# A delta rule, then Fourier mixing and an MLP, on one core: MLP pieces recorded inside the first mixing, and fewer beside the last batch's chain

## The chip, the cores and the metric

The kernel runs on one core of a Trainium2 chip. The metric is the device time of one execution in microseconds (us). Six runs are given, and their median is the number that a change is held against. One further execution was profiled; its trace is what is read below.

The core's engines run side by side, each through its own instruction list in order, and wait for one another by semaphores. In the profile PE is TensorE (matmuls, with PEld its weight loads), DVE is VectorE, ACT is ScalarE, POOL is GpSimd, and SP is the engine that issues most DMA transfers.

## The reference

Two blocks follow each other, on 4 batches, 8 heads, 768 rows and a head dimension of 48 (so 384 columns):

```python
k_n = k / (np.linalg.norm(k, axis=-1, keepdims=True) + 1e-06)
for t in range(S):
    y[:, :, t] = np.einsum('bhd,bhde->bhe', q[:, :, t], state)
    v_old = np.einsum('bhde,bhd->bhe', state, kt)
    state = state + bt[:, :, :, None] * np.einsum('bhd,bhe->bhde', kt, vt - v_old)
...
X = np.fft.fft(x, axis=1)
X = np.fft.fft(X, axis=2)
mixed = np.real(X).astype(np.float32)
u = x + mixed
un = (u - mu) / np.sqrt(var + 1e-06)
ch = np.maximum(un @ w_ch1, 0.0) @ w_ch2
return (u + ch).astype(np.float32)
```

The second block takes `y` with the heads side by side as `x`. The two weights (384 x 1536 and 1536 x 384) come as 64-bit floats, and the kernel turns them into 32-bit ones itself. All arithmetic is in 32-bit floats; a matmul of this kind is two records in the trace.

## The kernel before

**The recurrence as a chain.** Rows are taken in chunks of 64: 12 chunks to a batch, 48 chain steps in all (`chain`, L657). A step is three rounds that each need the one before: products of the state with the keys (`pc<-st`) and a subtraction on DVE (`U<-V,pc`); products with a small triangular inverse (`pc<-U,wt`) and a copy on ACT (`U<-pc`); products with the keys (`pc<-U,kp`) and an addition on DVE (`st<-st,pc`). After every second step `outputs` (L715) forms 128 rows of the first block's result in `x` (`py` products, an ACT copy, a DVE addition).

**Ahead of the chain.** Four steps are a quad, eight a group. For each group `prepare` (L413) transposes keys and queries (`pt`) and forms their products (`pg`), `invert` (L500) inverts 32 x 32 triangles for 128 partitions at once on DVE (a transpose into `X`, some 60 small operations named `A<-X` and `X<-X,A`, then `Y`, `Z` and a transpose back into `A`), and `merge` (L626) joins them into the `wt` tiles by `pj` products and ACT copies. A step can't use its `wt` before its group is merged.

**Behind the chain.** `fourier` (L777) mixes a finished batch: folds on DVE and POOL (into `hT` or `scr`, and `F`), products with the Fourier tables (`pf`), an ACT copy into `F`, then for each of three tiles the products `pb`, six DVE additions into `x`, the statistics (`bst`, `mv`) and the reciprocal deviation `rstd` on POOL; the third tile has one more product, `pd`. Each `yield` in it ends one recorded step. The first mixing has 15 such steps, a later one 13. When a tile's `rstd` is recorded, its key stands in `norms`. `mlps` (L900) is the MLP, over twelve pairs (batch, tile) in a row: normalise into `un` (DVE), transpose (`ptr`, ACT copy into `unT`), 12 pieces of three `ph` matmuls with an ACT copy into `hT`, 12 pieces of two `po` matmuls in two rows, each row closed by a DVE addition into `x` and a store. Each yield is a recorded step. A step comes back empty when the next pair isn't in `norms`, or when the second weight isn't yet converted for the next `po` (`converted`). The second weight's conversion (`second_weight`, L358) uses ACT (`digits`, L300), two DVE operations and one on POOL per piece of 128 rows, with three stage buffers that DMAs on SP refill.

**What sets the order.** Up to chain step 11 the order is written out by hand (`strict[0] = True`). From L1096 on, a scheduler at build time orders each engine's list, by the order of recording as priority and by which inputs and buffers it holds ready; at run time each list is followed as built. So what the main loop (L1131 to L1172) records earlier tends to stand earlier. Beside each chain step it adds to two counters. Each of the three rounds adds `PRE` (or 4.6 for the first group) to the one for the preparation of the next group, and `SIDE[b]` to the one for the MLP; when that one reaches 1, `beside` (L1123) records one step of the current mixing, if one is under way, and one MLP step. While a step waits to be merged, `beside` is called as well. After the last step the last mixing is begun and `beside` is called until all is recorded. The first mixing's two first steps are recorded beside chain steps 10 and 11, its other 13 in one go at chain step 12, by `run(first_mixing)` (L1154).

The PSUM buffers named "one" (two of them) serve `pt`, `ptr`, `pf`, `pb`, `pd`, `ph` and `po` in turn.

Of the kernel before, what the change touches and what calls it, by code (L numbers as in the profile page):

```python
# [82 lines left out]
def kernel(  # L83
# [542 lines left out]
    def merge(g):  # L626

        for lh in range(2):
            M = Merge(g, lh)
            for step in range(2):  # L630
                for half in range(2):
                    M.products(step, half)
                yield "ACT"
                M.taken(step, vs=(0,))
                yield "ACT"
                M.taken(step, vs=(1,))
                for hh in range(2):
                    yield ("ACT", "DVE")[step]
                    M.diagonal(step, hh, *((), (dve.tensor_copy,))[step])
                if step == 0:  # L640
                    yield
            merged.add(2 * g + lh)
            yield
# [110 lines left out]
    def advancing(gens):  # L754

        if gens and next(gens[0], "end") == "end":
            gens.pop(0)
# [17 lines left out]
    norms = {}  # L775
# [192 lines left out]
    def advance(gen, n=1):  # L968
        for _ in range(n):
            if next(gen, "end") == "end":  # L970
                return False
        return True

    def run(*gens):
        for gen in gens:
            for _ in gen:
                pass
# [5 lines left out]
    def queries(*Qs):  # L983
        for Q in Qs:
            while Q >= NB and Q - NB in held:
                yield
            yield from prepare(Q, (1,))
# [69 lines left out]
    first_mixing = fourier(0)  # L1057
# [40 lines left out]
    def kept(gen):  # L1098

        while True:  # L1100
            strict[0] = True
            more = advance(gen)
            strict[0] = False
            if not more:
                return
            yield

    def ahead(g):
        if g == 2:
            yield from kept(queries(4, 5))  # L1110
        for Q in (2 * g, 2 * g + 1):
            while Q >= NB and Q - NB in held and g > 2:
                yield
            if g > 2:
                yield from prepare(Q)
        yield from invert(g)
        for _ in merge(g):
            yield

    mixing = [None]  # L1120
    channels = mlps()

    def beside():  # L1123

        if mixing[0] is not None:
            if not advance(mixing[0]):
                mixing[0] = None
        return advance(channels)


    PRE, SIDE = 2.4, (0.0, 1.5, 2.2, 2.2)  # L1131
    pre, due = ahead(2), [0.0, 0.0]
    for m in range(NCH, STEPS):
        b, n = divmod(m, NCH)
        g, Q = m // (2 * QT), m // QT

        count = 0
        while Q not in merged:
            advance(pre)
            count += 1  # L1140
            if count % 3 == 0 and b > 1 or count % 4 == 0 and len(converted) == KF:
                beside()
        if m % (2 * QT) == 1:
            run(pre)
            pre = ahead(g + 1) if g + 1 < NG else iter(())
            due = [0.0, 0.0]
        for i, _ in enumerate(chain(m)):
            if i < 2:
                advancing(later)
            if n == 0 and i == 1:  # L1150
                run(*later)
                later.clear()
                if b == 1:
                    run(first_mixing)  # L1154
                else:
                    mixing[0] = fourier(b - 1)
            if b == 1 and (n > 0 or i > 1):
                advance(second, 3)
            if m > NCH or i > 0:
                due[0] += 4.6 if g == 1 else PRE  # L1160
                due[1] += SIDE[b]
            while max(due) >= 1.0:
                if due[1] >= 1.0:
                    due[1] -= 1.0
                    beside()
                if due[0] >= 1.0:
                    due[0] -= 1.0
                    advance(pre)
# [34 lines left out]
```

## Time and profile before

| what | value |
|---|---|
| median of six runs | 777.41 us (773.63 to 780.0) |
| profiled execution | 773.58 us, span 771.9 us |
| mean granted PE clock | 0.982 of full speed |
| `ph` matmuls | 864 records, 209.9 us busy |
| `po` matmuls | 576 records, 209.3 us busy |
| chain step 12 / 16 / 36 / 40 / 47, first product | 153.3 / 215.6 / 489.2 / 554.2 / 629.1 us |

The span runs from the first to the last instruction; the execution's own time has a little around it. The page gives busy time by engine, the chain of waits that ended last, and groups of instructions; windows give the same busy times for a stretch, and a timeline lists instructions in order with, in brackets, the idle time before one and what ended it. The granted clock is the share of full speed that PE's clock was given: matmuls take longer where it is below 1. A busy PE is not the same as a PE at full speed, and idle time on an engine that nothing waits for costs nothing.

### The profile page before, as it was taken

The numbers are of one execution on the slowest core, as the hardware profiler recorded it, in microseconds if no ns is written. First come the engines' busy times: TensorE is split into PE (matmuls) and PEld (weight loads), VectorE is DVE, ScalarE is ACT, GpSimd is POOL, SyncE is SP. The second block draws the span as 40 slices with busy tenths as digits, with TensorE's granted clock in tenths as the row PEclk, the third lists the DMA queues.
The fourth block names the chain that finished last, engine by engine and source line by source line (L and its number), as shares of the span: only waits on it lengthen the run. The fifth ranks groups of instructions, "written<-read, shape, count | busy, mean of one in ns | idle before, by whom it ended". The sixth has DMA issues, their size and how long they took to land.

```text
span 771.9 us, 18290 instructions
## 1 busy us (share of the span) xinstructions
PE 678.7 (88%) x7768; PEld 486.1 (63%) x7768; DVE 395.6 (51%) x980; ACT 258.1 (33%) x700; POOL 80.5 (10%) x116
## 2 busy tenths in 40 slices
PE   5934598887979898899999999899999999799996
PEld 4622477665746665766766667567667676577683
DVE  2599776889972597344894123889211114600000
ACT  3742355543336414523313544113522122121120
POOL 8010023323000000000100000101000001100000
PEclk9999999998999999999999999899999999899999
DMA  8642032343112201002202010000100000000000
GB/s 182 166 108 50 6 85 65 87 141 74 31 27 49 45 14 44 11 12 42 48 11 48 7 33 17 16 11 11 23 23 2 21 2 21 0 1 21 10 11 20
DMA packets 81041, 30.78 MB, mean 40 GB/s; under 512 B 75856, under 2 KB 77392, under 8 KB 80960
## 3 DMA queue, kind: packets, MB, share of 16 engines
q1 hardware_dynamic: 76560, 21.92, 13.3%
q0 software_dynamic: 2224, 7.31, 2.9%
q8 instruction: 61, 1.00, 0.5%
q10 hardware_dynamic: 2176, 0.39, 0.3%
q14 instruction: 20, 0.16, 0.1%
HBM read 24.87 MB, written 4.72 MB: 38 GB/s over the span
## 4 chain that ended last, share of the span: by engine, by line
PE 54%; DVE 26%; ACT 6%; DMA 5%; SPq 4%; issue 3%; POOL 1%; POOLq 0%; DVEq 0%; ACTq 0%
PE ph L131 18%; PE po L131 17%; DVE A L131 6%; DVE X L131 5%; PE pc L131 5%; DVE x L131 3%; DVE w L131 3%; PE pf L131 3%; ACT A L131 2%; PE pj L131 2%; PE pg L131 2%; PE pt L131 2%; SPq L219 2%; DMA qp<-in_q_dram 2%; PE pb L131 2%
## 5 line engine op out<-in xcount | busy, mean ns | idle before, releaser
L131 PE MATMUL ph<-unT,w 128*128 128x256 f32 x864 | 209.9, 392 | 2.8 <-DVE x L131 1.4
L131 PE MATMUL po<-w,hT 128*128 128x384 f32 x576 | 209.3, 504 | 0.0
L131 PEld LDWEIGHTS ph<-unT,w 128*128 128x128 f32 x864 | 160.4, 192 | 30.7 <-ACT unT L131 2.2
L131 PEld LDWEIGHTS po<-w,hT 128*128 128x128 f32 x576 | 103.9, 192 | 61.1 <-issue 4.1
L131 ACT ACTIVATE hT<-ph 128x256 f32<-128x256 f32 x144 | 55.0, 382 | 189.3 <-PE ph L131 189.1
L131 DVE TENSOR_TENSOR x<-x,po 128x384 f32<-128x384 f32 x24 | 13.2, 552 | 95.4 <-PE po L131 95.3
L131 PE MATMUL pg<-KQT 48*64 48x64 f32 (+1 forms) x1152 | 45.1, 299 | 6.4 <-ACT KQT L131 4.6
L770 POOL DMA_INDIRECT out_dram<-x,rows_hi x12 | 12.3, 1026 | 353.8 <-DVE x L131 223.0
L131 DVE TENSOR_TENSOR U<-V,pc 128x192 f32<-128x192 f32 x48 | 16.7, 348 | 63.4 <-PE pc L131 63.4
L131 PEld LDWEIGHTS pg<-KQT 48*64 48x64 f32 x1152 | 34.6, 180 | 22.9 <-ACT KQT L131 12.3
L131 ACT ACTIVATE KQT<-pt 128x256 f32<-128x256 f32 (+1 forms) x84 | 33.0, 413 | 45.7 <-PE pt L131 44.8
L131 DVE TENSOR_TENSOR X<-X,A 128x30 f32<-128x30 f32 (+14 forms) x120 | 40.7, 339 | 3.2
L131 DVE TENSOR_TENSOR A<-X 128x30 f32<-128x30 f32 (+14 forms) x120 | 39.6, 330 | 3.1
L131 DVE TENSOR_TENSOR st<-st,pc 128x192 f32<-128x192 f32 x44 | 15.4, 350 | 49.5 <-PE pc L131 31.5
L131 ACT ACTIVATE U<-pc 128x192 f32<-128x192 f32 x48 | 15.8, 329 | 65.5 <-PE pc L131 62.1
L131 PE MATMUL pt<-pack,qp 128*128 128x128 f32 x96 | 23.7, 344 | 15.5 <-DMA qp<-in_q_dram 12.1
L131 PEld LDWEIGHTS pc<-U,wt 64*64 64x64 f32 x768 | 20.9, 154 | 22.9 <-DVE U L131 9.2
L131 PE MATMUL pc<-U,wt 64*64 64x48 f32 x768 | 28.0, 250 | 7.5 <-DVE U L131 5.5
L131 PEld LDWEIGHTS pc<-st,KQT 48*64 48x64 f32 x768 | 18.9, 157 | 24.8 <-DVE st L131 11.8
L131 DVE TENSOR_TENSOR x<-x,pb 128x191 f32<-128x191 f32 (+1 forms) x72 | 25.0, 411 | 18.4 <-PE pb L131 18.4
L131 PE MATMUL pc<-st,KQT 48*64 48x48 f32 x768 | 25.6, 252 | 8.8 <-DVE st L131 8.5
L131 PE MATMUL pt<-pack,kp 128*128 128x128 f32 x96 | 24.2, 360 | 6.7 <-DMA pack<-k_pack 4.7
(135 smaller groups left out, 831.6 us busy)
## 6 DMA issues: line engine op xcount, KB each, us to landing
x<-in_moe_w_ch_dram SPq DMA_DIRECT2D x14, 384.0 KB, 3.9
qp<-in_q_dram SPq DMA_DIRECT2D x96, 48.0 KB, 2.4
kp<-in_k_dram SPq DMA_DIRECT2D x80, 48.0 KB, 2.4
V<-in_v_dram SPq DMA_DIRECT2D x56, 48.0 KB, 2.4
w<-in_moe_w_ch_dram POOLq DMA_DIRECT2D x6, 384.0 KB, 8.3
x<-in_moe_w_ch_dram POOLq DMA_DIRECT2D x4, 384.0 KB, 7.9
V<-in_v_dram SPq DMA_DIRECT2D x64, 24.0 KB, 2.2
out_dram<-x SPq DMA_DIRECT2D x8, 192.0 KB, 1.9
```

Of the source, the lines that this page charges most:

```text
L131: ins = getattr(self.engine, name)(*args, **kwargs)
L219: eng.dma_start(out=vals[Q][64 * p:64 * p + CH, cs, u, :], in_=v[b, 4 * (p ^ (u % 2)) + u, t0:t0 + w * CH, :].rearrange("(c p) d -> p c d" ...
L770: nc.gpsimd.indirect_dma_start(out=out.rearrange("b s m -> (b s) m"), out_offset=bass.IndirectOffsetOnAxis(ap=rows_hi[:, i:i + 1], axis=0) ...
```

## The change

Two edits in the main loop. The remaining 13 steps of the first mixing are still recorded at chain step 12, but one at a time; once the first tile's statistics are recorded, two MLP steps are recorded after each further mixing step. And the rate of MLP steps beside the last batch's chain is 1.8 a round where it was 2.2.

```diff
-    PRE, SIDE = 2.4, (0.0, 1.5, 2.2, 2.2)
-    pre, due = ahead(2), [0.0, 0.0]
+    PRE, SIDE = 2.4, (0.0, 1.5, 2.2, 1.8)
+    pre, due, started = ahead(2), [0.0, 0.0], False
...
                 if b == 1:
-                    run(first_mixing)
+                    while advance(first_mixing):
+                        if (0, 0) in norms or started:
+                            started = advance(channels, 2)
                 else:
                     mixing[0] = fourier(b - 1)
```

`advance(gen, n)` (L968) takes `n` steps of a generator and says whether it goes on. `normalised`, in the first MLP step, takes the pair out of `norms`, so `started` keeps the loop recording MLP steps.

The recorded MLP steps, empty ones behind the stroke, counted by the chain step that the main loop was at:

| chain step | 12 | 13 | 14 | 15 | 35 | 36 | 37 | 38 | 39 | 47 | after |
|---|---|---|---|---|---|---|---|---|---|---|---|
| before | 3 | 4 | 5 | 4 | 6 | 7 | 7 | 6 | 7 | 7 | 82 / 2 |
| changed | 15 | 3 / 1 | 2 / 3 | 4 | 6 | 4 / 2 | 2 / 3 | 6 | 5 | 5 | 94 |

The scheduler takes this up in the built lists. Between the first products of neighbouring chain steps PE's list holds these MLP pieces (three `ph` or two `po` matmuls each):

| chain step | 13 | 14 | 15 | 16 | 17 | 35 | 36 | 37 | 38 | 39 |
|---|---|---|---|---|---|---|---|---|---|---|
| before | 5 | 5 | 5 | 6 | 3 | 6.5 | 6.5 | 5 | 6 | 10 |
| changed | 5 | 12 | 6 | 5 | 4 | 6.5 | 3.5 | 0 | 6 | 6 |

## The prediction

> **What bounds the kernel now.** I read the page's busy totals first, then its chain that ended last, then the windows of five stretches, then the timelines inside them.
>
> ```profile
> PE 678.7 (88%) x7768; PEld 486.1 (63%) x7768; DVE 395.6 (51%) x980; ACT 258.1 (33%) x700; POOL 80.5 (10%) x116
> ...
> PE 54%; DVE 26%; ACT 6%; DMA 5%; SPq 4%; issue 3%; POOL 1%; POOLq 0%; DVEq 0%; ACTq 0%
> ```
>
> PE (TensorE) has the most work and over half of the chain; DVE (VectorE) has a quarter of it. Where each decides, the windows tell (columns: stretch; length, busy time of PE, weight loads, DVE, ACT, POOL with instruction counts; granted PE clock, DMA share, GB/s).
>
> ```profile
> 170.00:236.00 66.00, 55.16 (x725) 37.87 (x724) 55.03 (x151) 25.68 (x73) 8.75 (x12) 0.95 0.22 52
> 236.00:476.00 240.00, 227.88 (x2773) 159.67 (x2773) 121.02 (x314) 93.81 (x268) 12.14 (x15) 0.99 0.15 30
> 476.00:540.00 64.00, 60.00 (x587) 41.85 (x579) 57.59 (x157) 14.29 (x36) 6.92 (x10) 0.95 0.06 13
> 540.00:642.00 102.00, 101.80 (x1140) 70.18 (x1141) 15.82 (x38) 27.38 (x82) 2.02 (x2) 1.00 0.05 15
> 642.00:672.00 30.00, 23.27 (x109) 16.40 (x108) 16.80 (x49) 5.16 (x10) 4.45 (x7) 0.89 0.02 7
> ```
>
> Five stages: the first mixing and the inversion for chain steps 16 to 23 (170 to 236: PE idle 10.8 us, DVE nearly full); a PE-bound stretch (12.1 us idle in 240); the third mixing beside the last inversion (476 to 540: PE idle 4.0, DVE nearly full too); the last batch's chain, where PE is never free; and the last mixing (6.7 us idle). After 672 PE runs solid to 765.7, and a store ends the span. PE's work is the same before and after, so the sum is the change of PE's idle time plus what a lowered clock costs.
>
> **The change, part by part.** One MLP piece (a recorded step of MLP work: six ph or four po records) costs 1.30 us of PE: the profile's chain has 72 ph in 15.54 and 48 po in 15.63 us, twelve pieces each. Both halves only move pieces; they add none. I counted them in the recording and in the built order of each engine. The first half records 12 MLP steps inside the first mixing. Later, one step at chain step 13 and three at 14 come back empty, because the second weight isn't converted yet. So 8 pieces, 10.4 us of PE work, run ahead from step 14 on. The built order keeps that lead up to step 35.
>
> *First mixing (gain 3 us).* The price of putting 10.4 us more beside steps 13 to 16 lies between 0 hidden (or 2 us lost) and all 10.4 hidden. The slack is 10.8 idle plus 2.75 of clock:
>
> ```profile
> 176.00:180.00 4.00, 1.90 (x24) 1.18 (x28) 3.94 (x13) 0.77 (x2) 0.93 (x2) 0.70 0.05 9
> 180.00:184.00 4.00, 3.95 (x32) 2.86 (x29) 3.97 (x13) 1.75 (x4) 2.22 (x3) 0.50 0.37 67
> ...
> 187.93 1.01 ACT L131 ACTIVATE x<-x 128x384 int32<-128x384 uint32 x2 [0.90 <-DMA x<-in_moe_w_ch_dram]
> ```
>
> (1.90 x 0.30 + 3.95 x 0.50 + 4.0 x 0.05 = 2.75.) But the new order brings waits of its own. U of step 13 now stands before tiles 1 and 2 on DVE, and PE's second product of step 13 before their pb products: PE waits for it from 170.2 to about 172.8, then for the tile's rstd (POOL, ended at 174.1) some 1.4 us. The hT copies stand on ACT behind the second weight's digit copies, which wait for DMAs as in the row above, 1.5 to 2.5 us. And ph, ptr, pb and pd share two PSUM buffers; a pb holds one through six DVE adds (2.07 us), so about eight ph pieces lose 0.5 us each.
>
> The end of this stage is set by DVE's list, from the first tile's mean at 172.35 to the last transpose A at 225.1: 52.8 us. In the changed list one po add comes in (0.55), and step 16's V scaling and U (0.96 + 0.35) fall behind A: with the old waits out (0.97 + 0.24 + 0.45) that is 50.4. New waits, placed by the PE times above: 0.7 and 0.7 for two rstd, 0.5 and 1.0 for pb of tiles 1 and 2, 1.5 for pd, 1.7 for LQ masks and U of step 15: 6.1, so 56.5. The list ends near 229, and step 16's second product comes about 3.5 us later. At that product 24 po and 3 ph matmuls stand in the new order against 16 po in the old one: 8 x 0.65 + 3 x 0.43 = 6.5 us of work ahead. Net gain 6.5 - 3.5 = 3.0. DMA order: SP's store of the first tile now stands between the V loads of steps 16 to 19 and waits for the add at step 15; five V loads at 0.7 us to issue and 2.4 to land still end near 229, before DVE reads V near 231. If the add slips by more than 2 us, that scaling is late, and step 16 behind it.
>
> *Steps 17 to 35 (0).* Same rate, same lead; reshuffling may cost or save 2 us.
>
> *Third mixing (loss 10.4 us).* Here the lead is spent. In steps 36 to 38 five MLP calls come back empty, since all MLP work of batches 0 and 1 is done and batch 2 has no norms, and the lower rate records three fewer. The built order puts 3.5, 0 and 6 pieces into steps 36, 37 and 38, where 6.5, 5 and 6 stood. Over steps 36 to 38 the lead of 8 falls to 0. Were PE the bound, the chain would come 10.4 us earlier for it; but DVE carries the inversion (X, 476.5, to A, 539.2) and the mixing, 57.6 busy in 64. Its waits for other engines there sum to 4.2 us, the most a freer PE could give back. Against that stands this:
>
> ```profile
> 489.17 0.68 PE L131 MATMUL pc<-st,KQT 48*64 48x48 f32 x16 [2.25 <-DVE st L131]
> ...
> 488.00:492.00 4.00, 2.83 (x20) 1.83 (x21) 3.21 (x11) 0.00 (x0) 0.00 (x0) 0.52 0.18 31
> 492.00:496.00 4.00, 4.00 (x22) 1.96 (x22) 3.73 (x10) 0.00 (x0) 0.00 (x0) 0.62 0.00 0
> ```
>
> One idle gap of 2.25 us, and the granted clock is 0.52 and 0.62 for the next 8 us. With nothing beside the pf and pb products, such gaps come twice more, and the mixing's own products slow from 2.8 to about 5 us a group on the path to DVE's adds. I let the two cancel: 10.4, with 6.4 and 14.4 as its ends.
>
> *Last batch (0.3).* 1.8 for 2.2 takes 0.4 x 3 x 1.30 = 1.6 us from each step. A step took 10.7 us (554.2 to 629.1 over seven), so 9.1 remain, against 5 to 6 us for a bare step (steps 1 to 9: 92.1 to 132.0). PE stays the bound, and the work only goes behind the chain.
>
> *Last mixing (gain 2.7 us).* Before, the MLP pieces run out in the middle of it, and batch 3's first piece waits for norms:
>
> ```profile
> 645.47 1.70 PE L131 MATMUL pf<-stab,scr 128*128 128x65 f32 x12 [0.48 <-DVE scr L131]
> ...
> 661.95 0.59 PE L131 MATMUL ptr<-pack,un 128*128 128x128 f32 x3 [3.74 <-DVE un L131]
> ...
> 664.61 2.93 PE L131 MATMUL ph<-unT,w 128*128 128x256 f32 x6 [0.58 <-ACT unT L131]
> ...
> 664.00:668.00 4.00, 3.42 (x10) 2.83 (x10) 1.25 (x5) 0.86 (x2) 0.92 (x2) 0.50 0.01 2
> ```
>
> Idle 6.7 and, in the windows from 660 to 672, clock about 2.5 (1.47 x 0.22 + 3.42 x 0.50 + 3.53 x 0.14): 9.2 lost. After, 15 ph and 24 po matmuls, 22 us, fill it to the end. But only three ph, 1.3 us, stand between the chain's last product and the first pf, which comes 4.6 us after it (640.9 to 645.5): 3.3 idle, longer than the gap that halved the clock, so 3 more, and 0.2 of small waits: 6.5. Gain 9.2 - 6.5 = 2.7; bounds 1 and 7.
>
> [...]
>
> Sum: -3.0 + 0 + 10.4 + 0.3 - 2.7 = +5.0 us on the profiled execution's 773.58 (span 771.9), so 778.6. The median of the runs, 777.41, lies 3.83 above that execution; the same offset gives 782.4.
>
> **The rivals.**
>
> *Faster: the holes are really filled.* If the pieces fill the first mixing's slack to 9 of 10.4, DVE gets back 2 of its 4.2 us at the third mixing, and the last mixing saves 6: -9 + 10.4 - 2 - 6 = -6.6, 770.8 as a median. For it: PE does idle 10.8 us there. Against it: DVE's list, not PE, ends that stage, and the new waits. It decides from the point where first and last mixing together save 10.4 us and what DVE doesn't give back.
>
> *Nothing to see.* 5 saved at first, 4.5 at last, 10.4 lost: +0.9, 778.3. For it: all that is lost was first gained, as pieces move from one hole to another. Against: the first hole closes only in part.
>
> *Much slower: ACT's queue.* hT copies stand behind digit copies, those behind DMAs that wait for POOL's joins, those behind DVE. If each of three turns adds 2 us, the inversion ends so much later that nothing is gained at first: 0 gained, 2 more for chain steps that come late, 10.4 lost, 0 at last as its gap is longer: +12.4, 789.8. For it: 187.93 above. Against: the digit operations on DVE also come earlier in the new order (U13 at 172.4 instead of 181.3).
>
> *That the change doesn't do what it says* I exclude: the counts show the 12 steps, and a tail of 94 recorded MLP steps where 84 stood.
>
> **How the numbers follow.** Forecast 0.48, nothing to see 0.22, faster 0.20, much slower 0.10. The forecast's own range is 778.5 to 787. The whole range reaches to both rivals: 771 to 791, with a bit over one in ten left below and less than one above. 0.5% is 3.9 us, about what a measurement of this kernel can tell from no change: slower than 781.3 holds 0.40 of the forecast and all of the last rival, 0.50; faster than 773.5 nearly all of the faster case, 0.19; the rest, 0.31, lies within.
>
> **What would show it.** First mixing: PE idle between 170 and 236 near 8 to 11 us, not 3; the last A transpose near 229. Steps 36 to 38: almost no po beside pf and pb, PE idle 12 to 16 us in the 64 that begin with X (476.5 before), granted clock well below 0.95, DVE's stretch from X to A still about 62 us. Last mixing: po between the pb products, no wait for un, one gap of about 3 us ahead of the first pf. Wrong I would be if the inversion for steps 16 to 23 ended by 225 with the lead in hand, or if X to A at the third mixing shrank by over 4 us.

## The result, and the profile after

| | before | changed |
|---|---|---|
| median of the runs made side by side | 777.47 us (771.67 to 781.78) | 787.17 us (781.59 to 788.56) |
| ratio to before, 95% interval | | 1.0112 [1.0094, 1.0129] |
| span of the profiled execution | 771.9 us | 782.2 us |
| mean granted PE clock | 0.982 | 0.971 |

The changed kernel is slower by 9.7 us of the medians, 8.7 by the ratio. The forecast was +5.0 us and a median of 782.4, so its direction and its range (771 to 791) hold, and its size is about half.

First the changed kernel's page: the busy totals, and the chain that ended last, by engine.

```profile
PE 687.4 (88%) x7768; PEld 492.9 (63%) x7768; DVE 395.1 (51%) x980; ACT 258.1 (33%) x700; POOL 83.9 (11%) x116
...
PE 61%; DVE 25%; ACT 7%; issue 3%; DMA 2%; POOL 1%; POOLq 0%; ACTq 0%; SPq 0%; DVEq 0%
```

The instruction counts are those of before. Yet PE is busy 8.7 us longer (687.4 for 678.7), and idle only 1.6 us longer (782.2 - 687.4 = 94.8, for 771.9 - 678.7 = 93.2). So nearly all of the lost time appears as slower matmuls, and hardly any as idle time.

The windows of the changed kernel, cut where the same five stages lie now (stretch; length, busy PE, weight loads, DVE, ACT, POOL with counts; granted clock, DMA share, GB/s). The last line is the third mixing's inversion alone, from `X` to `A`; before, that took 62.70 us with PE busy for 58.70 of them at a clock of 0.95.

```profile
170.00:236.00 66.00, 58.35 (x584) 39.92 (x585) 54.74 (x149) 22.69 (x63) 10.67 (x12) 0.90 0.21 49
236.00:486.00 250.00, 238.33 (x2936) 166.87 (x2934) 121.17 (x314) 98.84 (x284) 13.12 (x15) 0.99 0.14 29
486.00:554.00 68.00, 58.65 (x594) 41.68 (x586) 57.65 (x160) 13.62 (x33) 7.44 (x10) 0.87 0.09 19
554.00:640.00 86.00, 82.97 (x1030) 56.40 (x1020) 14.94 (x35) 24.48 (x74) 3.02 (x3) 0.98 0.03 11
640.00:682.00 42.00, 37.94 (x161) 27.07 (x162) 19.28 (x56) 5.93 (x12) 4.46 (x9) 0.92 0.03 10
486.30:552.90 66.60, 57.25 (x544) 40.69 (x545) 56.32 (x156) 12.57 (x30) 7.44 (x10) 0.87 0.09 19
```

DVE does the same 56.3 us of work between `X` and `A` as before (56.33), but the stretch is 3.9 us longer. PE's busy time fell by only 1.45 us, although 5.4 pieces fewer (20.4 for 25.8), 7.0 us of work, begin in it. Most of the rest went to the clock, 0.87 for 0.95: it was at 0.50 for 17.1 us of the stretch, where it had been for 6.8, and half of the difference, 5.1 us, is missing at full speed.

**Where the time went.** A chain step's start alone says little, because the changed kernel has done more MLP work by then. So I take from each start the lead, at 1.30 us a piece, and cut the span at the first product of step 35. The lead there is 8 pieces.

| | before | changed | changed, lead taken out |
|---|---|---|---|
| start to step 35 | 475.8 | 485.5 | 475.1 (-0.7) |
| step 35 to the end | 296.1 | 296.7 | 307.1 (+11.0) |

After step 35 the changed kernel has 10.4 us less to do and takes 0.6 us more. By stages the 11.0 are: up to step 40, the first that needs the last inversion, +10.5 (it begins at 558.8 for 554.2, with 4 pieces fewer done instead of 8 more: 4.6 + 5.2 + 0.7); the last batch, +2.0 (step 47 at 627.9 for 629.1, 10 pieces fewer done); last mixing and tail, -1.5.

What the third mixing looks like now, first PE's timeline of the changed kernel (start, length, instruction and count; in brackets the idle time before it and what ended it):

```profile
498.96 0.68 PE L131 MATMUL pc<-st,KQT 48*64 48x48 f32 x16 [1.56 <-DVE st L131]
...
510.43 4.05 PE L131 MATMUL pf<-stab,scr 128*128 128x65 f32 x24 [1.85 <-DVE scr L131]
...
528.11 0.52 PE L131 MATMUL ptr<-pack,un 128*128 128x128 f32 x3 [2.98 <-DVE un L131]
```

then the same kernel's windows around two of these gaps:

```profile
496.00:500.00 4.00, 2.44 (x39) 1.57 (x36) 3.59 (x15) 0.00 (x0) 0.00 (x0) 0.74 0.29 74
500.00:504.00 4.00, 4.00 (x18) 1.71 (x20) 3.31 (x9) 0.00 (x0) 0.00 (x0) 0.50 0.14 24
...
528.00:532.00 4.00, 2.73 (x9) 1.94 (x10) 4.00 (x14) 0.98 (x2) 0.00 (x0) 0.58 0.02 4
532.00:536.00 4.00, 4.00 (x13) 2.98 (x12) 0.81 (x3) 0.38 (x1) 1.12 (x2) 0.56 0.00 0
```

and DVE's waits in this stage of the changed kernel (total us, times, longest):

```profile
DVE x L131 <- PE pb L131: 4.5, 2, 3.3
```

with the same group in the kernel before:

```profile
DVE x L131 <- PE pb L131: 0.8, 1, 0.8
```

Read together: PE runs dry three times, for 1.56, 1.85 and 2.98 us, and about each of these gaps its clock goes down to 0.50 (behind the second one from 512 to 515 us). The mixing's `pb` products come later, and DVE, which carries the inversion, waits 4.5 us for them instead of 0.8. These 3.7 us are nearly all of the 3.9 by which the inversion grew. How much of them is clock isn't shown: ahead of the last `pb` products PE's list also holds two groups of `ptr` and a piece of `ph`, which wait for DVE and ACT.

### The profile page after: what moved, and what is told of

It is laid out like the page before. It is cut to its first block, busy times and chain, and to the rows that moved or that the text cites. A ratio compares the mean times of both kernels' runs of the same rounds, so it can differ in the third digit from the quotient of the medians.

```text
span 782.2 us, 18288 instructions
## 1 busy us (share of the span) xinstructions
PE 687.4 (88%) x7768; PEld 492.9 (63%) x7768; DVE 395.1 (51%) x980; ACT 258.1 (33%) x700; POOL 83.9 (11%) x116
## 4 chain that ended last, share of the span: by engine, by line
PE 61%; DVE 25%; ACT 7%; issue 3%; DMA 2%; POOL 1%; POOLq 0%; ACTq 0%; SPq 0%; DVEq 0%
PE ph L131 20%; PE po L131 18%; DVE A L131 6%; PE pc L131 5%; DVE X L131 5%; PE pf L131 4%; PE pg L131 3%; DVE x L131 3%; DVE w L131 3%; ACT A L131 3%; PE pj L131 2%; PE pt L131 2%; PE pb L131 2%; PE py L131 2%; ACT wt L131 2%
## 5 line engine op out<-in xcount | busy, mean ns | idle before, releaser
L131 PE MATMUL ph<-unT,w 128*128 128x256 f32 x864 | 212.2, 394 | 5.6 <-ACT hT L131 4.1
L131 PEld LDWEIGHTS po<-w,hT 128*128 128x128 f32 x576 | 106.1, 194 | 64.6 <-issue 5.7
L131 PEld LDWEIGHTS pc<-U,wt 64*64 64x64 f32 x768 | 19.4, 156 | 23.8 <-DVE U L131 10.4
L131 ACT ACTIVATE A<-pj 32x128 f32<-32x128 f32 (+1 forms) x76 | 20.7, 273 | 40.4 <-PE pj L131 39.6
L131 PE MATMUL pc<-U,wt 64*64 64x48 f32 x768 | 25.8, 251 | 7.7 <-DVE U L131 5.8
```

The costliest lines, as they stand in the source:

```text
L131: ins = getattr(self.engine, name)(*args, **kwargs)
```

## The experiments

"Rate" below is `SIDE`. Each ratio is against the kernel before, on the same chip. The spans of the profiled executions are split in the manner shown above: "head" is step 35's start less the lead, "rest" is from there to the end plus the lead, both as differences from the kernel before.

| kernel | median | ratio | lead at 35 | head | rest |
|---|---|---|---|---|---|
| changed | 787.17 | 1.0112 [1.0094, 1.0129] | +8 | -0.7 | +11.0 |
| e1_first_half | 792.39 | 1.0172 [1.0136, 1.0208] | +8 | +3.4 | +17.8 |
| e2_second_half | 775.46 | 0.9970 [0.9948, 0.9991] | 0 | +5.0 | -1.1 |
| e3_lead_kept | 772.81 | 0.9923 [0.9894, 0.9953] | +2 | +1.7 | -2.4 |
| e4_dummy | 782.32 | 1.0065 [1.0033, 1.0097] | +8 | -0.8 | +7.6 |
| e5_spread_only | 772.70 | 0.9957 [0.9922, 0.9991] | -6 | +0.1 | -2.5 |
| e6_warm_first | 768.81 | 0.9883 [0.9844, 0.9922] | +2 | 0.0 | -3.5 |
| e7_warm_last | 767.74 | 0.9882 [0.9841, 0.9922] | +2 | -0.4 | -5.5 |
| e8_one_go | 773.29 | 0.9954 [0.9928, 0.9980] | +2 | +1.9 | -2.6 |
| e9_spread_warm | 774.17 | 0.9944 [0.9915, 0.9973] | -6 | +0.6 | -2.1 |
| e10_third_warm | 774.96 | 0.9947 [0.9915, 0.9978] | +2 | +1.7 | -0.5 |
| e11_warm_36 | 773.92 | 0.9943 [0.9914, 0.9973] | +2 | +4.7 | -5.3 |

Before any is read, the noise of this split: up to step 35 e2 has the same lists as the kernel before, and its head came out 5.0 us later. A head that differs by less says nothing. Head and rest are those of one execution each and don't add up to the difference of the medians: the profiled execution of the kernel before was 3.8 us faster than the median of 777.41, those of e1 and e2 were 2.5 and 2.1 slower than their own medians. Stages behind step 17 repeat better: from step 40 to 47, e3, e6, e7, e8 and e11, with the same lists there, all took 66.4 us.

**The two halves alone.** e1 is the change without its second edit, e2 without its first:

```diff
-    PRE, SIDE = 2.4, (0.0, 1.5, 2.2, 1.8)
+    PRE, SIDE = 2.4, (0.0, 1.5, 2.2, 2.2)
```

> Only the MLP steps inside the first mixing; the rate beside the last batch stays 2.2. Spent lead (mine: 8 pieces run ahead from step 14 and are missing beside the third mixing at steps 36 and 37): most of the loss is here, +6 to +10 us against the kernel before, and steps 36 and 37 again hold 3.5 and 0 MLP pieces. Rate (the lower rate beside the last batch is what costs): within 3 us of the kernel before.

```diff
-    pre, due, started = ahead(2), [0.0, 0.0], False
+    pre, due = ahead(2), [0.0, 0.0]
...
-                    while advance(first_mixing):
-                        if (0, 0) in norms or started:
-                            started = advance(channels, 2)
+                    run(first_mixing)
```

> Only the rate of 1.8; the first mixing is recorded as before. Spent lead: no MLP call is empty at steps 36 and 37, so 0 to +5 us against the kernel before (three pieces fewer beside the third mixing, a little saved at the last). Rate: +6 to +10 us.

The first half alone costs 13.4 us (1.72% of 778.38), more than the whole change and more than the 6 to 10 us expected; the second alone gains 2.3, where 0 to 5 us of loss were expected. The signs decide between the two branches, the sizes were missed. So all of the loss is the first half's, and the second takes part of it back. In e1 the MLP again runs out in the last mixing, as PE's timeline of e1 shows:

```profile
671.15 4.66 PE L131 MATMUL pf<-stab,scr 128*128 128x64 f32 x24 [2.51 <-DVE scr L131]
...
683.25 0.87 PE L131 MATMUL ptr<-pack,un 128*128 128x128 f32 x3 [3.75 <-DVE un L131]
```

There are no pieces beside these products, and 6.3 us of idle time stand in front of them. The other reason for its size is the first mixing: up to step 17 e1's lists are those of the changed kernel, but step 17 began at 247.3 us instead of 243.3. The windows of the changed kernel there

```profile
176.00:184.00 8.00, 8.00 (x42) 5.61 (x41) 5.15 (x17) 1.52 (x4) 1.70 (x4) 0.50 0.30 98
184.00:192.00 8.00, 8.00 (x53) 6.48 (x53) 7.50 (x19) 2.67 (x7) 5.22 (x4) 1.00 0.08 14
```

and those of e1

```profile
176.00:184.00 8.00, 6.54 (x39) 4.71 (x40) 4.49 (x13) 1.74 (x4) 3.20 (x4) 0.50 0.31 87
184.00:192.00 8.00, 8.00 (x44) 6.30 (x44) 7.21 (x20) 3.02 (x8) 3.87 (x3) 0.73 0.10 25
```

differ in where the clock came back: at once after 184, or later in that window.

**Is it the lead, spent at the wrong place?** e3 keeps both edits and lowers the rate beside batch 2, where PE is the bound, so that six of the eight early pieces are paid back there:

```diff
-    PRE, SIDE = 2.4, (0.0, 1.5, 2.2, 1.8)
+    PRE, SIDE = 2.4, (0.0, 1.5, 2.0, 1.8)
```

> The changed kernel with a rate of 2.0 instead of 2.2 beside the third batch (chain steps 24 to 35), so that the lead is spent there, where PE is the bound, and steps 36 to 38 hold 4.5, 5 and 4 MLP pieces instead of 3.5, 0 and 6. Spent lead: 6 to 12 us faster than the changed kernel, within -4 to +3 us of the kernel before. Rate, or a loss made by the new order in the first mixing itself: within 3 us of the changed kernel, +6 to +11 us against the one before.

One number, and the loss is gone: 14.4 us less than the changed kernel's median (6 to 12 were expected), and faster than before. Steps 36 to 38 now hold 4.5, 5 and 4 pieces and no MLP call comes back empty. The inversion from `X` to `A` takes 61.9 us; with the changed kernel's 9.5 pieces in these steps it took 66.6, with the 17.5 of before 62.7. More telling is the time from step 35's first product to step 40's, beside the pieces that the built lists hold there, and how long after the inversion's end step 40 begins:

| kernel | e10 | before | e2 | e5 | e3 | e4 | changed | e1 |
|---|---|---|---|---|---|---|---|---|
| pieces in steps 35 to 39 | 35 | 34 | 30 | 29 | 28 | 22 and 5 unused | 22 | 28 |
| step 35 to step 40, us | 80.3 | 78.4 | 75.2 | 72.9 | 70.3 | 73.0 | 73.3 | 84.9 |
| `X` to `A`, us | 61.6 | 62.7 | 64.7 | 62.2 | 61.9 | 64.6 | 66.6 | 70.3 |
| end of `A` to step 40, us | 17.9 | 15.0 | 9.8 | 9.4 | 7.7 | 7.7 | 5.9 | 13.8 |

From 35 pieces down to 28 the stage gets shorter by 10.0 us, 1.4 a piece, about what a piece costs. The inversion doesn't follow it (61.6 to 64.7 us); what shrinks is the rest of the chain's work between its end and step 40. At 28 pieces little of that is left. The stage repeats well: e6, e7, e8 and e11, with e3's pieces in these steps, took 70.2 to 70.5 us, and e9, with e5's lists, 73.1. The changed kernel has six pieces fewer still, its step 40 follows the inversion at 5.9 us, and there is nothing more to win; the inversion itself has grown instead. So its 12 pieces fewer than before (15.6 us) bring 5.1 us (78.4 to 73.3): 7.5 of the loss is work taken away beyond what e3 shows to come back (15.6 - 8.1), and 3.0 is the distance to e3's 70.3. How dear a dry step can be is seen in e1: with e3's 28 pieces, but none or few at steps 36 and 37, it takes 14.6 us more.

**Is it work or clock?** e4 is the changed kernel with three unused `ph`-size matmuls wherever an MLP step comes back empty after the second weight is converted. They fill PE, but do no work:

```diff
-        return advance(channels)
+        said = next(channels, "end")
+        if said is None and converted.issuperset(range(KF)):
+            ph = ps_one([128, GT * 128], "ph")
+            for dt in range(KD):
+                mm(ph, w1[:, dt, 0:128], w1[:, dt, 0:GT * 128], dt == 0, dt == KD - 1)
+        return said != "end"
```

> The changed kernel with three matmuls of ph's size (their result is used by nothing) recorded in each of the five MLP calls that come back empty beside the third mixing: 6.5 us of PE work more, no work done. Spent lead with half of the loss by PE's slowed clock on DVE's path: the stretch from X to A at the third mixing falls from 66.6 to 61 to 64 us, and the kernel is 2 to 5 us faster than the changed one. Missing work alone: as the changed kernel within 2 us. Clock alone: 8 to 10 us faster than the changed kernel.

The median fell by 4.9 us, and the span by 3.5. From `X` to `A` the clock is 0.95 again, and the stretch 64.6 us; but step 40 comes no earlier (73.0 us after step 35, for 73.3), as fillers take PE's time too, and PE still ran dry for 3.57 us ahead of a `pf` product. So a mended mean clock alone doesn't bring the stage back. How much of the 3.0 us above e3 is clock and how much waits in the uneven order, this run doesn't tell. What it gained lies behind the stage, where its lists are again those of the changed kernel: 1.7 us from step 40 to 47 (67.4 for 69.1), as the clock stayed at 1.00 behind the merge, and 1.4 from step 47 on (152.9 for 154.4), as the clock was low for 3.4 us instead of 6.8 behind the same gap of 3.15 us. So the 2 to 5 us of the first branch came true, but not by its mechanism, the shorter inversion.

**What are the early pieces worth?** e5 is the kernel before with e3's rates, so without them. e8 has them, but recorded in one go behind the first mixing:

```diff
-                    while advance(first_mixing):
-                        if (0, 0) in norms or started:
-                            started = advance(channels, 2)
+                    run(first_mixing)
+                    advance(channels, 12)
```

> The first mixing recorded as before the change, with the rates 2.0 and 1.8 of the run before (lead kept). Spent lead (the early pieces are worth the idle time that they fill, some 3 us, once they are spent where PE is the bound): 1 to 5 us slower than the run with the lead kept. Rates alone (the early pieces are worth nothing, and lower rates are what made that run fast): within 2 us of it, or faster.

> The run with the lead kept, but with the first mixing recorded in one go and the same 12 MLP steps after it, so that only the place of recording differs. Spent lead (pieces count, not their place between the tiles): within 3 us of the run with the lead kept. Order (the tiles of the first mixing behind MLP pieces are what delays step 13 and slows the clock): 3 to 6 us faster, and chain step 17 begins before 242 us.

e5 and e3 can't be told apart (0.9957 and 0.9923, intervals overlapping), and so it is with e8 and e3; in e8 step 17 began at 246.1 us, not before 242. That a loan is paid back without loss beside batch 2 is seen from step 17 to step 35: the changed kernel, e1 and e4, with the same lists, took 242.3 us each; e3, e6, e7, e8 and e10, with six pieces fewer there, 234.2 to 235.8, so 1.1 to 1.3 us a piece. PE is the bound there. The rates bring the gain; the mixing recorded tile by tile, the part of the change that its description puts first, brings nothing that I could measure, in one form or the other.

**Filling the short gaps.** e6, e7, e9, e10 and e11 put unused matmuls (`warm`, on a tile `pw`) in front of a gap, to see what the low clock after it costs. e7 has seven before the last mixing, e6 six at the first:

```diff
+    def warm(times):
+        pw = ps_one([128, GT * 128], "pw")
+        for i in range(times):
+            mm(pw, w1[:, 0, 0:128], w1[:, 0, 0:GT * 128], i == 0, i == times - 1)
...
-    PRE, SIDE = 2.4, (0.0, 1.5, 2.2, 1.8)
+    PRE, SIDE = 2.4, (0.0, 1.5, 2.0, 1.8)
...
+    warm(7)
```

> The run with the lead kept, plus seven matmuls of ph's size, used by nothing, recorded between the chain's last products and the last mixing, where PE waits some 3 us for the first fold. Clock: the granted clock from 640 to 648 us of the changed kernel's trace (0.66 and 0.50) stays at 1.0 in that stage here, and the kernel is 2 to 4 us faster. Idle gap alone: no change within 1 us.

In e3 the last mixing began so, by PE's timeline

```profile
630.67 0.66 PE L131 MATMUL pf<-stab,scr 128*128 128x65 f32 x2 [3.15 <-DVE scr L131]
```

and by its windows

```profile
628.00:632.00 4.00, 1.33 (x4) 1.26 (x5) 1.71 (x6) 0.00 (x0) 1.52 (x2) 0.79 0.00 0
632.00:636.00 4.00, 4.00 (x16) 3.46 (x15) 0.00 (x0) 0.85 (x2) 0.00 (x0) 0.50 0.00 0
```

in e7, by its timeline

```profile
623.80 3.29 PE L131 MATMUL pw<-w 128*128 128x256 f32 x14
```

and by its windows

```profile
624.00:628.00 4.00, 4.00 (x19) 3.51 (x19) 1.65 (x4) 0.42 (x1) 1.58 (x2) 1.00 0.00 0
628.00:632.00 4.00, 3.87 (x29) 3.31 (x28) 1.49 (x6) 1.63 (x4) 0.00 (x0) 1.00 0.00 0
```

The gap was closed by work that nobody needs, the clock stayed at 1.00, and step 47 to the end took 151.3 us instead of 154.4. That this is the clock's price is seen in kernels whose lists are the same from step 47 on but for the filler: with the clock at 0.50 for 6.8 us (e3, e8) this stretch took 154.4 and 154.3 us, with 3.4 us of it (e6) 153.3, with none (e7, e11) 151.3. With e6, from which it can't be told apart, this is the fastest kernel found: 767.74 us, 0.9882 [0.9841, 0.9922].

> The run with the lead kept, plus six matmuls of ph's size, used by nothing, recorded in front of the first MLP step inside the first mixing, where PE otherwise waits some 2.6 us for U of chain step 13 and its clock halves. Clock on the path: the granted clock from 176 to 184 us rises from 0.50 to above 0.8, the inversion's last transpose ends 2 to 4 us earlier, and the kernel is 1 to 4 us faster than with the lead kept. DVE's list alone sets that stage's end: within 1 us, or slower by up to the 2 us of matmuls.

e6 is faster than e3 by a like amount, but not as meant: the wait for `U` was gone, the one of 1.68 us for `un` was not, the clock from 176 to 184 was still 0.66, and step 17 began at 242.6 us, inside the 242.4 to 247.3 of kernels with the changed order and no such filler. Inconclusive.

> The first mixing as before the change, the rates 2.0 and 1.8, and the seven matmuls in front of the last mixing: the run before with matmuls in front of the last mixing, without the early pieces. Early pieces worth nothing: within 2 us of that run (767.7 us). Early pieces worth the 3 us of the prediction: 2 to 5 us slower.

e9 is e5 with `warm(7)` as in e7. Step 47 to the end: 163.1 us for 162.9 in e5, no gain. The gap it should have filled was only 1.77 us in e5, followed by 3.4 us of the clock at 0.50. In e9 the clock stayed at 1.00; the 1.7 us that this saves are about what 3.29 us of filler cost in such a gap. By the ratios e9 is 4.8 us slower than e7, as the second branch had it, but the intervals touch, and 3.4 of the 4.4 us between the two spans lie behind step 35. So this run doesn't show that early pieces are worth it, nor that they aren't.

e10 is e7 with more pieces beside the last batch's first four steps:

```diff
-                due[1] += SIDE[b]
+                due[1] += 2.4 if b == 3 and n < 4 else SIDE[b]
```

> The early pieces, 2.0 beside the third batch, 2.4 at chain steps 36 to 39 and 1.8 after them, and the matmuls in front of the last mixing: 7, 7, 7 and 7 recorded MLP steps at 36 to 39, as many as before the change. Missing work beside the third mixing still costs (three to five pieces fewer in the run with 2.0): 2 to 5 us faster than the run with matmuls in front of the last mixing alone. DVE's list sets that stage and the hole is closed already: within 2 us.

Not faster, but 5.1 us slower than e7 by the ratios. The inversion took 61.6 us as in e3, but step 40 began 80.3 us after step 35 instead of 70.3, for seven pieces more: the far end of the table above.

e11 is e7 with `warm(5)` ahead of the state product of steps 24 and 36, where the 1.56 us gap lay:

```diff
+            if b > 1:
+                warm(5)
```

> The run with matmuls in front of the last mixing, plus five matmuls of ph's size, used by nothing, in front of the first state product of chain steps 24 and 36, where PE waits about 2 us for the copy of the first state and its clock halves. Clock on the path: the granted clock stays at 1.0 in the 12 us behind chain step 36, and the kernel is 1 to 4 us faster than without them. DVE's list alone: within 1 us.

The scheduler put the filler behind the gap, not into it, as PE's timeline of e11 shows

```profile
496.51 2.42 PE L131 MATMUL pw<-w 128*128 128x256 f32 x10 [2.26 <-DVE st L131]
```

so the state product waited for it. Step 40 came 70.5 us after step 35 (e7: 70.3): where the inversion sets the end, the 2.4 us of filler cost next to nothing. The clock did stay at 1.00 from `X` to `A`, where e3 had 0.94, as the first branch wanted; but the inversion took 61.6 us for 61.9. So with 28 pieces in the stage, the low clock behind step 36 is worth next to nothing. From step 17 to 35, where the other group stands and PE is the bound, e11 took 239.5 us for e7's 235.6. That and 1.3 us before step 17 are the 5.1 by which its head is later; by the ratios e11 is 4.7 us slower than e7.

## Why the prediction was right, and which terms were off

On the profiled executions the change cost 10.3 us, 5.3 more than the forecast. Of these, 2.3 lie up to step 35, 0.1 in the third mixing, 1.7 in the last batch and 1.2 in the last mixing.

**First mixing and steps 17 to 35: predicted -3.0 and 0, measured -0.7 in one profile against one.** The mechanism was as told. PE waits 2.59 us for `U` (forecast: 2.6) and 1.68 for the tile's `rstd` (1.4), by PE's timeline of the changed kernel:

```profile
172.31 0.45 PE L131 MATMUL pc<-U,wt 64*64 64x48 f32 x16 [2.59 <-DVE U L131]
174.44 0.88 PE L131 MATMUL ptr<-pack,un 128*128 128x128 f32 x3 [1.68 <-DVE un L131]
```

The last transpose into `A` ended at 227.7 us (forecast near 229; 225.1 before), and PE's idle time in the stretch was 7.65 us (8 to 11). What the working lacked: it counted the low clock of before as slack that the pieces would fill, but behind these two waits the clock was 0.50 for a full 8 us (the row 176 to 184 above). The heads of equal lists (before and e2: 0 and +5.0; changed, e4 and e1: -0.7, -0.8, +3.4) spread by as much as the term, so whether it is -3 or 0 stays open.

**Third mixing: predicted +10.4, measured +10.5.** Right in size, and in its place: e3, which pays most of the lead back elsewhere, has no such loss. "I let the two cancel" is the step that was half wrong in its make-up. Against 10.4 I set a return of at most 4.2 us, as "DVE carries the inversion". But DVE sets step 40 only once the chain has caught up with the inversion; before, it was 15.0 us behind it, and down to 28 pieces PE's time comes back in full. On the other side more pieces were missing up to step 40 than I counted (12, as step 39 has 6 for 10), and starving cost 3.0 us. The term came out right by luck, because these nearly balance: 10.4 + 5.2 - 8.1 + 3.0 = 10.5. The marks show it: X to A was to stay near 62 us with PE idle for 12 to 16 of 64; they were 66.6 and 9.35 (66.60 - 57.25). The clock took much of what I had put down as idle time. That it alone made the inversion later isn't shown: in e4, at 0.95, it still took 64.6 us. That the inversion now sets step 40 is seen in PE's timeline of the changed kernel, where the merge has to wait for it:

```profile
557.59 0.69 PE L131 MATMUL pj<-A 32*64 32x64 f32 x32 [1.46 <-ACT A L131]
```

**Last batch: predicted +0.3, measured +2.0.** This is the mis-sized term. "PE stays the bound, and the work only goes behind the chain" left out what the merge's gap does to the clock behind it, in the changed kernel's windows:

```profile
560.00:564.00 4.00, 4.00 (x27) 2.02 (x26) 0.00 (x0) 1.35 (x6) 0.00 (x0) 0.65 0.02 4
```

4.0 x 0.35 = 1.4 us. e4 shows that this is the cause: from step 40 on its lists are the same, the gap before this merge was 0.63 us instead of 1.46, and the clock stayed at 1.00, by e4's windows:

```profile
560.00:564.00 4.00, 4.00 (x61) 2.21 (x59) 0.35 (x1) 0.93 (x4) 0.00 (x0) 1.00 0.00 0
```

There the last batch cost +0.3, as forecast (67.4 us with six pieces fewer than before, for 74.9). I priced seven steps by their mean and didn't look at the first of them, which has a wait in front.

**Last mixing: predicted -2.7, measured -1.5**, inside its bounds of -7 to -1. The gap ahead of the first `pf` was forecast at 3.3 us:

```profile
641.74 0.66 PE L131 MATMUL pf<-stab,scr 128*128 128x65 f32 x2 [3.15 <-DVE scr L131]
```

and it was to halve the clock for 3 us:

```profile
640.00:644.00 4.00, 2.26 (x8) 2.11 (x9) 1.71 (x6) 0.00 (x0) 0.60 (x2) 0.66 0.00 0
644.00:648.00 4.00, 4.00 (x19) 3.54 (x18) 0.33 (x1) 1.24 (x3) 0.00 (x0) 0.50 0.00 0
```

(2.26 x 0.34 + 4.0 x 0.50 = 2.8). The mixing's later holes are filled, but for one small one that the working left out: 1.41 us ahead of `pd`, where PE waits for DVE.

The clock was at 0.50 for 6.8 us, from 641.3 to 648.1, so this gap did act on it, as the one of 2.25 us at step 36 had in the kernel before. e7, which took the gap away and won 3.1 us against e3 from step 47 to the end (151.3 for 154.4), gives the price.

**The rivals.** Faster fell at the third mixing, where two of DVE's 4.2 us of waits were to come back and the inversion took 3.9 longer. Nothing to see fell on the last mixing (1.5 saved, not 4.5). ACT's queue didn't show: from 174 us on the digit copies found their data there when their turn came, and step 17 was 1.2 us early by the lead's measure, 7 pieces at that point (243.3 - 9.1 against 235.4). The time came close to that rival's 789.8 all the same, by other terms: +10.3 on the profiled span, from 10.5 + 2.0 - 1.5 - 0.7.

**Open.** Whether early pieces are worth anything once the rate is 2.0: e3 against e5 says no, and e7 against e9 (0.9882 and 0.9944, intervals overlapping) allows up to 5 us.

## What to carry to other kernels

Filler work that is moved ahead is a loan: what it is worth is decided where fewer pieces are then left. Taken from steps in which the filling engine is the bound, it comes back in full; taken until a step runs dry or another engine sets the end, it is lost and more. So count pieces per step in the built order, and spread what is left evenly (here a rate of 2.0 for 2.2 beside batch 2: 14 us between two medians). Price a starved stage by idle time and clock together, and look at each step that holds a wait rather than at the stage's mean.

## What the runs showed of the hardware that was not expected

- A gap of 1.5 us can be enough for the clock: in the changed kernel it was 0.65 behind 1.46 us (560 to 564), and 0.74 and then 0.50 around and behind 1.56 us (496 to 504). Yet the same gap doesn't always act. e3 and e7 have the same lists up to step 47, and both wait 1.35 us for the merge ahead of step 17. In e3, by its timeline and its windows, the clock was at half behind it for 3.4 us

```profile
232.18 0.69 PE L131 MATMUL pj<-A 32*64 32x64 f32 x32 [1.35 <-ACT A L131]
...
232.00:236.00 4.00, 3.82 (x69) 2.54 (x70) 1.68 (x4) 3.40 (x12) 0.00 (x0) 0.79 0.02 4
236.00:240.00 4.00, 4.00 (x72) 2.44 (x70) 0.55 (x1) 1.80 (x7) 1.13 (x1) 0.78 0.00 0
```

and in e7 it was not:

```profile
230.60 0.69 PE L131 MATMUL pj<-A 32*64 32x64 f32 x32 [1.35 <-ACT A L131]
...
232.00:236.00 4.00, 4.00 (x75) 2.85 (x74) 0.91 (x2) 2.91 (x11) 0.30 (x1) 1.00 0.01 4
```

- The length of a gap doesn't settle it. In the kernel before, the clock stayed at 1.00 around and behind a wait of 2.41 us in the same merge, by PE's timeline and the windows

```profile
223.36 0.69 PE L131 MATMUL pj<-Z,A 32*64 32x64 f32 x32 [2.41 <-DVE Z L131]
...
220.00:224.00 4.00, 1.59 (x36) 0.78 (x35) 3.93 (x3) 0.65 (x2) 0.00 (x0) 1.00 0.00 0
224.00:228.00 4.00, 2.56 (x34) 1.42 (x34) 3.79 (x10) 3.87 (x14) 0.00 (x0) 1.00 0.05 14
228.00:232.00 4.00, 3.63 (x82) 2.13 (x71) 0.17 (x1) 2.85 (x10) 0.00 (x0) 1.00 0.11 39
```

while the 2.25 us ahead of step 36 in the same trace were followed by 0.52 and 0.62. And at one gap of 3.15 us, the one ahead of the last mixing, the clock was at 0.50 for 6.8 us in the changed kernel, e3 and e8, and for 3.4 us in e4 and e6. Between 170 and 755 us the clock's records are 1.00 or 0.50 in the traces of before and changed (values between are means): 0.50 four times, for 23.9 us in all, before, and eight times, for 44.4 us, in the changed kernel. What else decides whether a gap acts isn't shown.

- Equal instruction lists spread by several us, in part by the clock: step 17 began between 242.4 and 247.3 us in kernels whose lists up to there are the changed kernel's. In the latest of them, e1, the clock had been at 0.50 for 13.7 us in the first mixing, in the changed kernel for 10.2. One profile against one can't settle a term of 3 us.
